# Linear attention with a decaying state, then top-128 expert routing: chunks of 64 tokens and 64x64x64 products instead of chunks of 128

## The chip, the core and the metric

The program runs on one core of a Trainium2 chip. The metric is the device time of one launch in microseconds. TensorE (PE) multiplies into PSUM, VectorE (DVE) and ScalarE (ACT) read PSUM, GpSimd (POOL) works on SBUF alone, and SyncE's queue (SP) issues nearly all transfers.

## What is computed

```python
B, H, S, D = 4, 8, 768, 64          # q, k, v; block = 64
for b in range(nb):
    intra = einsum('bhic,bhjc->bhij', qb, kb) * Dmask
    intra = einsum('bhij,bhjd->bhid', intra, vb)
    inter = einsum('bhid,bhde->bhie', qb * lam_pow, kv_state)
    out[:, :, sl] = intra + inter
    kv_state = lam_block * kv_state + einsum('bhsd,bhse->bhde', kb * rev_pow, vb)
x = out.transpose(0, 2, 1, 3).reshape(B, S, 512)
scores = einsum('bsd,d->bs', x, w_gate)
for b in range(B):                   # the 128 tokens with the highest score of each batch
    xe = x[b, top_idx]
    ye = maximum(xe @ w1, 0) @ w2    # 512 -> 1024 -> 512
    out[b, top_idx] = x[b, top_idx] + sigmoid(scores[b, top_idx])[:, None] * ye
```

All is float32. The chunk length is free, since the recurrence gives the same sums for any.

## The kernel before, in words

Tokens are worked in 24 tiles of 128 tokens (4 batches of 6), all 8 heads of a tile together. The order of every engine is the order in which the code is written (`manual_schedule`), and each engine takes its instructions strictly in that order. The loop over `g` at the end of the function is the pipeline. Step `g` issues the loads of tile `g+4` (three transfers of 256 KB, and in steps 0 to 3 two 512 KB pieces of the expert's weights as well), turns q and k of tile `g+2` round (`transposes`), takes the scores and the next state of tile `g+1` (`scores`, `next_state`), and the outputs of tile `g` (`outputs`). SP's queue holds the loads and the store of each tile in the same order.

Per tile, two heads make a pair `hp`. `scores` multiplies one head at a time: 64 rows of the array hold a head's keys, 128 columns its 128 tokens, and the two heads of a pair use the upper and the lower half of the array's rows. `mask` holds the powers of the decay for a 128x128 block. `next_state` multiplies keys by values for two heads at once and keeps the two useful 64x64 blocks of each 128x128 result; POOL decays the whole 128x512 state, zeros included, and DVE adds the blocks. `outputs` adds, per pair, one product with the state and two with the scores, in one PSUM bank `po`; ACT copies it to `x_b`, SP stores it, and DVE takes the gate's score (`xg`, `sc`).

`routing` ranks a batch's 768 scores once its last tile is done. PE spreads the scores over all partitions (`pb`), ACT copies them (`sc_row`), and DVE counts for every token how many come before it: two counting compares and a tie break for each of the 6 tiles (`count`, lines L265, L269, L273), three tiles in one step. `expert` then makes a 0/1 matrix out of the ranks (`pick`), PE turns it into row numbers (`pe`), POOL gathers the 128 rows (`xs`), and PE, ACT and DVE run the two layers (`gate` with `pt`, `hidden` with `ph`, `back` with `py` and `y`) before POOL scatters the rows back. `plan` spreads these pieces over the steps after the batch: counts at steps 6(b+1) and the next, `where` (pick and pe) 3 steps after 6(b+1), the gather one later, then `gate`, two `hidden`, two `back`, one a step. What is planned behind step 23 runs after the loop, with nothing beside it.

Of the kernel before, what the change touches and what calls it, by code (L numbers as in the profile page):

```python
# [17 lines left out]
def kernel(  # L18
# [18 lines left out]
    L = 128  # L37
    NT = S // L
# [5 lines left out]
    AHEAD = 4  # L44
# [4 lines left out]
    ld = ctx.enter_context(tc.tile_pool(name="ld", bufs=AHEAD + 3))  # L49
# [3 lines left out]
    ps_t = ctx.enter_context(tc.tile_pool(name="ps_t", bufs=1, space=PSUM))  # L53
    ps_s = ctx.enter_context(tc.tile_pool(name="ps_s", bufs=1, space=PSUM))
    ps_u = ctx.enter_context(tc.tile_pool(name="ps_u", bufs=1, space=PSUM))
    ps_o = ctx.enter_context(tc.tile_pool(name="ps_o", bufs=1, space=PSUM))
# [41 lines left out]
    mask = const.tile([128, H, L], FP32, name="mask")
    for h in range(H):
        nc.vector.tensor_tensor_scan(  # L100
            out=mask[:, h, :], data0=lam_b[:, h : h + 1].broadcast_to([128, L]),
            data1=ident[:], initial=0.0, op0=ALU.mult, op1=ALU.add,
        )

    kpow = const.tile([128, H], FP32, name="kpow")
    nc.vector.tensor_copy(kpow[:], mask[:, :, L - 1])  # L106
# [4 lines left out]
    for hh in range(2):  # L111
        r = slice(hh * 64, (hh + 1) * 64)
        nc.vector.tensor_copy(lam_p[r, :], lam_b[r, hh::2])
    qpow = const.tile([128, NHP, L], FP32, name="qpow")
    for hp in range(NHP):
        nc.vector.tensor_tensor_scan(
            out=qpow[:, hp, :], data0=lam_p[:, hp : hp + 1].broadcast_to([128, L]),
            data1=zero[:], initial=1.0, op0=ALU.mult, op1=ALU.add,
        )
    decay = const.tile([128, NHP, 128], FP32, name="decay")  # L120
    nc.vector.tensor_copy(decay[:], qpow[:, :, L - 1 : L].broadcast_to([128, NHP, 128]))

# [389 lines left out]
```

## Time and profile before

| | us |
|---|---|
| median of 3 runs | 250.05 (247.73 to 252.8) |
| the profiled execution | 248.36 |
| its span, first to last instruction | 246.7 |
| PE busy in it | 213.3 |
| DVE busy | 130.2 |
| POOL busy | 79.4 |
| ACT busy | 51.3 |
| mean granted TensorE clock | 0.939 of 2.4 GHz |

The profiled execution is one launch under the hardware profiler. Its time is 1.66 us longer than its span. Busy matmul time counts each pass until its result is out, and passes overlap, so PE's share says that it is seldom empty and not how fast it goes; the spacing of the passes tells that. A float32 matmul stands in the trace as two passes, each with its own weight load, so 16 passes are 8 matmuls.

### The profile page before, as it was taken

What the parts mean: (1) busy time and instruction counts of PE and PEld (TensorE: products, weight loads), DVE (VectorE), ACT (ScalarE), POOL (GpSimd) and SP (SyncE); (2) the same over time, 40 slices, a digit from 0 to 9 for tenths busy, and PEclk for the clock granted to TensorE, in tenths of its full rate; (3) what the DMA queues carried; (4) which work ended last, traced back from release to release, by engine and by line L of the source; (5) the groups of instructions that cost most, each with busy time, mean ns of one, the idle gap of its engine ahead of it and who ended that gap; (6) DMA issues with size and microseconds to landing.
All of it is one profiled execution on the core that took longest, in us unless ns stands there. A gap on an engine that the chain in (4) does not pass through costs nothing.

```text
span 246.7 us, 4281 instructions
## 1 busy us (share of the span) xinstructions
PE 213.3 (86%) x1664; PEld 182.8 (74%) x1664; DVE 130.2 (53%) x371; ACT 51.3 (21%) x97; POOL 79.4 (32%) x77
## 2 busy tenths in 40 slices
PE   1798998799877899999995999999997889817991
PEld 1598997589767799899682999899674877306940
DVE  4556453247999535299746244399644227821001
ACT  2312222223220123322120123412210022001000
POOL 1459641426644143254143144155131100030001
PEclk9999999799999799999998599999998899985897
DMA  6999999999955948917439159800101210020001
GB/s 130 218 228 250 224 299 279 284 257 249 239 134 115 214 115 179 203 24 170 113 59 213 43 127 201 188 27 18 44 30 55 88 43 0 0 79 9 0 0 43
DMA packets 80947, 31.99 MB, mean 130 GB/s; under 512 B 75680, under 2 KB 75680, under 8 KB 80928
## 3 DMA queue, kind: packets, MB, share of 16 engines
q1 hardware_dynamic: 80144, 29.63, 53.1%
q0 software_dynamic: 640, 2.10, 2.7%
q8 instruction: 13, 0.21, 0.4%
q14 instruction: 6, 0.05, 0.1%
q10 hardware_dynamic: 144, 0.00, 0.0%
HBM read 24.38 MB, written 7.34 MB: 129 GB/s over the span
## 4 chain that ended last, share of the span: by engine, by line
PE 53%; SPq 13%; DVE 11%; issue 10%; DMA 8%; ACT 2%; POOLq 1%
PE po L217 10%; SPq L68 10%; PE ph L360 9%; PE py L373 8%; PE ss L158 8%; DMA kn<-in_k_dram 7%; PE po L211 6%; PE pu L177 5%; PE tp_kT L133 3%; PE tp_qT L133 2%; DVE pick L299 2%; DVE p L164 2%; DVE cmp L269 2%; SPq L84 1%; DMA xs<-out_dram,tok 1%
## 5 line engine op out<-in xcount | busy, mean ns | idle before, releaser
L217 PE MATMUL po<-vn,p 128*128 128x64 f32 x384 | 53.5, 268 | 0.0
L141 POOL TENSOR_TENSOR qs<-qT,qpow 128x512 f32<-128x512 f32 x20 | 26.2, 1309 | 80.0 <-ACT qT L137 80.0
L217 PEld LDWEIGHTS po<-vn,p 128*128 128x128 f32 x384 | 51.4, 198 | 0.0
L164 DVE TENSOR_TENSOR p<-ss,mask 128x512 f32<-128x512 f32 x48 | 30.9, 685 | 25.2 <-PE ss L158 24.9
L211 PE MATMUL po<-state,qs 128*128 128x128 f32 x160 | 36.3, 310 | 0.8 <-ACT x_b L221 0.8
L221 ACT COPY x_b<-po 128x512 f32<-128x512 f32 x24 | 14.1, 587 | 104.7 <-PE po L217 104.7
L158 PE MATMUL ss<-qT,kT 64*128 64x128 f32 x384 | 32.9, 314 | 2.4 <-DVE p L164 2.2
L360 PE MATMUL ph<-xsT,w_sb 128*128 128x128 f32 x256 | 32.8, 291 | 1.4 <-ACT xsT L335 1.4
L360 PEld LDWEIGHTS ph<-xsT,w_sb 128*128 128x128 f32 x256 | 31.7, 206 | 2.1 <-ACT xsT L335 2.0
L158 PEld LDWEIGHTS ss<-qT,kT 64*128 64x128 f32 x384 | 27.4, 212 | 7.3 <-issue 3.8
L224 DVE CUSTOM_DVE_ANT_0 xg<-x_b,wg_b 128x512 f32<-128x512 f32 x24 | 17.1, 711 | 26.9 <-ACT x_b L221 26.6
L373 PE MATMUL py<-w_sb,hs 128*128 128x512 f32 x64 | 28.7, 596 | 0.0
L211 PEld LDWEIGHTS po<-state,qs 128*128 128x128 f32 x160 | 25.6, 202 | 1.7 <-issue 1.5
L177 PE MATMUL pu<-vn,kd 128*128 128x128 f32 x160 | 24.3, 297 | 0.6 <-DVE state L193 0.6
L145 POOL TENSOR_TENSOR kd<-kn,kpow 128x512 f32<-128x512 f32 x20 | 21.4, 1071 | 8.6 <-DVE kpow L106 5.4
L384 POOL DMA_INDIRECT out_dram<-y,tok x4 | 4.1, 1014 | 59.0 <-DVE pick L299 36.8
L177 PEld LDWEIGHTS pu<-vn,kd 128*128 128x128 f32 x160 | 20.4, 200 | 3.3 <-issue 0.8
L133 PE MATMUL tp_qT<-ident,qn 128*128 128x128 f32 x96 | 16.1, 294 | 7.7 <-DMA qn<-in_q_dram 7.7
L187 POOL TENSOR_TENSOR state<-state,decay 128x512 f32<-128x512 f32 x16 | 21.3, 1330 | 1.1 <-DVE state L193 1.1
L269 DVE TENSOR_SCALAR_CACHE_REDUCE cmp<-sc_row,sc 128x768 f32<-128x768 f32 (+5 forms) x24 | 16.2, 675 | 9.7 <-ACT sc_row L250 9.7
L373 PEld LDWEIGHTS py<-w_sb,hs 128*128 128x128 f32 x64 | 11.7, 190 | 12.4 <-issue 12.4
L137 ACT COPY qT<-tp_qT 128x512 f32<-128x512 f32 x24 | 14.1, 586 | 28.4 <-PE tp_qT L133 28.3
(56 smaller groups left out, 171.6 us busy)
## 6 DMA issues: line engine op xcount, KB each, us to landing
qn<-in_q_dram SPq DMA_DIRECT2D x24, 256.0 KB, 4.5
kn<-in_k_dram SPq DMA_DIRECT2D x24, 256.0 KB, 5.1
vn<-in_v_dram SPq DMA_DIRECT2D x24, 256.0 KB, 5.0
out_dram<-x_b SPq DMA_DIRECT2D x24, 256.0 KB, 2.2
w_sb<-in_moe_w_dram SPq DMA_DIRECT2D x8, 512.0 KB, 5.9
wg_b<-in_moe_w_gate_dram SPq DMA_DIRECT2D x1, 256.0 KB, 5.3
xs<-out_dram,tok POOLq DMA_INDIRECT x4, 3.4
out_dram<-y,tok POOLq DMA_INDIRECT x4, 2.8
```

Of the source, the lines that this page charges most:

```text
L68: nc.sync.dma_start(out=t[:], in_=src[b, :, rows, :].rearrange("h p d -> p h d"))
L133: nc.tensor.transpose(tp[:, hp, :], in_=t[:, 2 * hp : 2 * hp + 2, :], identity=ident[:])
L141: nc.gpsimd.tensor_tensor(out=qs[:], in0=qTs[g][:], in1=qpow[:], op=ALU.mult)
L145: nc.gpsimd.tensor_tensor(out=kd[:], in0=kn[:], in1=kpow[:].unsqueeze(2).broadcast_to([128, H, D]), op=ALU.mult,)
L158: nc.tensor.matmul(ss[hh][:, hp, :], lhsT=kT[r, hp, :], rhs=qT[r, hp, :], start=True, stop=True,)
L164: nc.vector.tensor_tensor(out=p[:, hh::2, :], in0=ss[hh][:], in1=mask[:, hh::2, :], op=ALU.mult)
L177: nc.tensor.matmul(pu[:, hp, :], lhsT=kd[:, 2 * hp : 2 * hp + 2, :], rhs=vn[:, 2 * hp : 2 * hp + 2, :].rearrange("p h e -> p (h e)"), star ...
L187: nc.gpsimd.tensor_tensor(out=new[:], in0=states[g][:], in1=decay[:], op=ALU.mult)
L211: nc.tensor.matmul(po[:, 2 * hp : 2 * hp + 2, :].rearrange("p h e -> p (h e)"), lhsT=qs[:, hp, :], rhs=state[:, hp, :], start=True, stop=F ...
L217: nc.tensor.matmul(po[:, h, :], lhsT=p[:, h, :], rhs=vn[:, h, :], start=(c == 0), stop=True, skip_group_check=True,)
L360: nc.tensor.matmul(ph[:, i, :], lhsT=w1_sb[:, dc, fs], rhs=xsT[:, dc, :], start=(dc == 0), stop=(dc == NDC - 1),)
L373: nc.tensor.matmul(py[:], lhsT=hs[:, fc, :], rhs=w2_sb[:, fc, :], start=(fc == 0), stop=(fc == NFC - 1),)
```

## The change

Three things change. First, the recurrence runs over chunks of 64 tokens, two to a tile. Every attention product becomes 64x64x64, one for each head and chunk, on one quarter of the array: a half of the rows (`hh` or the chunk) and a half of the columns. The four quarters of a pair are written one behind the other. There are now 16 matmuls of that shape for each of scores, state, state times queries and scores times values. Second, a state is stored as 128x256 without the zero blocks, and a tile has two state updates. Scores and state products of a step share one PSUM tile `su` of two banks with one buffer; `po` has two banks, the odd heads of the two chunks crossed over, so that ACT needs three copies for it. The transposes share the two buffers `pm` with the expert's tiles. Third, one compare a tile counts the rank, after all scores of a batch were rounded to a coarser grid by adding and taking off a constant (`steps`), and one instruction makes `pick`. The pieces are planned anew: the routing of batches 0 to 2 begins a step later, two counts a step, `back` in one piece, and an expert's pieces begin after those of the one before.

```diff
-    AHEAD = 4
+    AHEAD = 6
...
+    def quarters():
+        for hp in range(NHP):
+            for hh, c in ((0, 0), (1, 1), (1, 0), (0, 1)):
+                yield hp, hh, c
...
+    def scores(g, su):
...
+        for hp, hh, c in quarters():
+            nc.tensor.matmul(
+                su[half[c], hh, 0, hp, :], lhsT=kT[half[hh], hp, half[c]],
+                rhs=qT[half[hh], hp, half[c]], start=True, stop=True, skip_group_check=True,
+            )
...
+    def masked(g, su):
+        p = att.tile([128, 2, NHP, C], FP32, name="p")
+        nc.vector.tensor_tensor(
+            out=p[:].rearrange("p a b i -> p a (b i)"),
+            in0=su[:, :, 0].rearrange("p a b i -> p a (b i)"),
+            in1=mask[:].rearrange("p a b i -> p a (b i)"), op=ALU.mult,
+        )
...
+    def state_products(g, su):
+        vn, kd = loaded[g][2], kds.pop(g)
+        for hp, hh, c in quarters():
+            if c == 1 and g % NT == NT - 1:
+                continue
+            h = 2 * hp + hh
+            nc.tensor.matmul(
+                su[half[hh], c, 1, hp, :], lhsT=kd[half[c], h, :], rhs=vn[half[c], h, :],
+                start=True, stop=True, skip_group_check=True,
+            )
+
+    def decay_state(n):
...
+        t = att.tile([128, NHP, D], FP32, name="decayed", bufs=2)
+        nc.gpsimd.tensor_tensor(out=t[:], in0=states[n][:], in1=decay[:], op=ALU.mult)
...
+    def next_state(n, su):
...
+            nc.vector.tensor_tensor(out=new[:], in0=u, in1=decayed.pop(n)[:], op=ALU.add)
...
+    def from_states(g):
...
+                po[half[hh ^ c], hh, hp * D : (hp + 1) * D],
+                lhsT=qs[half[hh], hp, half[c]], rhs=states[n][half[hh], hp, :],
+                start=(hp == 0), stop=False, skip_group_check=True,
+            )
...
+    def from_scores(g):
...
+                po[half[hh ^ c], hh, hp * D : (hp + 1) * D],
+                lhsT=p[half[c], hh, hp, :], rhs=vn[half[c], 2 * hp + hh, :],
...
+        nc.scalar.copy(out=x_b[:, t, :, 0, :], in_=po[:, 0])
+        for c in range(2):
+            nc.scalar.copy(out=x_b[half[c], t, :, 1, :], in_=po[half[1 - c], 1])
...
                 nc.vector.scalar_tensor_tensor(
...
+                    out=cmp[:], in0=keep["sc_row"][:], scalar=scs[b][:, t : t + 1],
+                    in1=earlier[:, (NT - 1 - t) * L : (NT - 1 - t) * L + S],
+                    op0=ALU.subtract, op1=ALU.is_gt, accum_out=keep["rank"][:, t : t + 1],
                 )
...
+            nc.vector.tensor_tensor(
+                out=pick[:],
+                in0=slots[:, r0 : r0 + 128].unsqueeze(1).broadcast_to([128, NT, 128]),
+                in1=rank[:].unsqueeze(2).broadcast_to([128, NT, 128]), op=ALU.is_equal,
+            )
...
-        s = (b + 1) * NT
+        s = (b + 1) * NT + (b < B - 1)
...
-            put(s + i // 3, piece)
+            put(s + i // 2, piece)
...
+        start_su(g)
+        su = sus.pop(g)
         if g + 2 < NG:
-            transposes(g + 2)
+            decay_state(2 * g + 4)
+        if g + 3 < NG:
+            keys_decayed(g + 3)
+        from_scores(g)
+        outputs(g)
         if g + 1 < NG:
-            scores(g + 1)
-            next_state(g + 1)
-        outputs(g)
+            from_states(g + 1)
+            scores(g + 1, su)
+        if g + 2 < NG:
+            state_products(g + 2, su)
+        if g + 1 < NG:
+            masked(g + 1, su)
+        if g + 2 < NG:
+            next_state(2 * g + 4, su)
+            decay_state(2 * g + 5)
+        gate_scores(g)
+        if g + 2 < NG:
+            next_state(2 * g + 5, su)
+        if g + 3 < NG:
+            transposes(g + 3, "qT", qTs)
+            queries_decayed(g + 3)
         if g % NT == NT - 1:
             plan(g // NT)
         for piece in later.pop(g, []):
             piece()
+        if g + 3 < NG:
+            transposes(g + 3, "kT", kTs)
```

In this code `half[i]` is partitions or tokens 64i to 64i+63, a chunk `n` is half a tile, and the work between two chunks is a chain: state products on PE, the add on DVE, the decay on POOL, the next add.

A step on PE, before (tp are the transposes, ss the scores, pu the state products, po the outputs; the four rows of the ss pair and of po that repeat are left out):

```order
L133 MATMUL tp_qT<-ident,qn 128x128 x4
L133 MATMUL tp_kT<-ident,kn 128x128 x4
L158 MATMUL ss_1717<-qT,kT 128x128
L158 MATMUL ss_1718<-qT,kT 128x128
...
L177 MATMUL pu<-vn,kd 128x128 x4
L211 MATMUL po<-state,qs 128x128
L217 MATMUL po<-vn,p 128x64 x2
```

And now, with the numbers-to-rows step of batch 1 in it (step 16; su holds scores and state products, pick and pe turn the ranks into row numbers):

```order
L243 MATMUL po<-vn,p 64x64 x16
L230 MATMUL po<-state,qs 64x64 x16
L176 MATMUL su<-qT,kT 64x64 x16
L196 MATMUL su<-vn,kd 64x64 x16
L154 MATMUL tp_qT<-ident,qn 128x128 x4
L337 LDWEIGHTS pick
L337 MATMUL pe<-place,pick 128x2
...
L154 MATMUL tp_kT<-ident,kn 128x128 x4
```

A step's 56 passes become 136. The transposes of tile g+3 end the step instead of beginning it, and pe stands between its two halves, where before it stood ahead of both.

DVE at the routing of a batch (batch 2), before (p is the masked scores, xg the gate's score):

```order
L260 MEMSET parts 128x1
L269 TENSOR_SCALAR cmp,parts<-sc_row,sc 128x768
L273 SCALAR_TENSOR_TENSOR cmp,parts<-sc_row,sc,below 128x128
L265 TENSOR_SCALAR cmp,parts<-sc_row,sc 128x128
L269 TENSOR_SCALAR cmp,parts<-sc_row,sc 128x640
L273 SCALAR_TENSOR_TENSOR cmp,parts<-sc_row,sc,below 128x128
L265 TENSOR_SCALAR cmp,parts<-sc_row,sc 128x256
L269 TENSOR_SCALAR cmp,parts<-sc_row,sc 128x512
L273 SCALAR_TENSOR_TENSOR cmp,parts<-sc_row,sc,below 128x128
L164 TENSOR_TENSOR p<-ss_1633,mask 128x4x128
L164 TENSOR_TENSOR p<-ss_1634,mask 128x4x128
```

And now (batch 0):

```order
L217 TENSOR_TENSOR state<-su,decayed 128x256
L315 TENSOR_SCALAR sc<-sc 128x6
L305 SCALAR_TENSOR_TENSOR cmp,rank_1154<-sc_row,sc,earlier 128x768 x2
L183 TENSOR_TENSOR p<-su,mask 128x512
L217 TENSOR_TENSOR state<-su,decayed 128x256
L267 ISA xg,sc<-x_b,wg_b 128x512
L267 ISA sc 128x1
L217 TENSOR_TENSOR state<-su,decayed 128x256
L305 SCALAR_TENSOR_TENSOR cmp,rank_1154<-sc_row,sc,earlier 128x768 x2
```

Between the masked scores of two steps stood eight counting instructions, and now stand two.

PE where the loop ends, before (the last rows of the attention, then the expert of batch 2):

```order
L211 MATMUL po<-state,qs 128x128
L217 MATMUL po<-vn,p 128x64 x2
L331 MATMUL pt<-ident,xs 128x128 x4
L360 MATMUL ph<-xsT,w_sb 128x128 x16
L245 MATMUL pb<-ident,sc 128x128 x6
L360 MATMUL ph<-xsT,w_sb 128x128 x16
L373 MATMUL py<-w_sb,hs 128x512 x8
```

And now:

```order
L176 MATMUL su<-qT,kT 64x64 x16
L337 LDWEIGHTS pick
L337 MATMUL pe<-place,pick 128x2
...
L243 MATMUL po<-vn,p 64x64 x16
L363 MATMUL pt<-ident,xs 128x128 x4
L288 MATMUL pb<-ident,sc 128x128 x6
L392 MATMUL ph<-xsT,w_sb 128x128 x32
L403 MATMUL py<-w_sb,hs 128x512 x8
```

Batch 2's pe stood two tiles ahead of the last outputs, before the scores of tile 23 (not shown). Now 16 matmuls, the outputs of tile 23, stand between it and pt, which needs the gathered rows.

## Rows read from the trace of the kernel before

**Rows 1.** Stretches: length; busy PE, PEld, DVE, ACT, POOL; clock; DMA share; GB/s.

```profile
0.00:63.90 63.90, 54.28 (x471) 49.15 (x472) 32.81 (x89) 16.94 (x30) 30.20 (x34) 0.97 1.08 243
63.90:81.80 17.90, 13.60 (x121) 11.95 (x119) 17.26 (x48) 3.73 (x7) 8.07 (x6) 1.00 0.69 154
81.80:131.80 50.00, 49.62 (x411) 43.32 (x410) 28.52 (x78) 12.39 (x24) 17.10 (x15) 0.97 0.62 136
131.80:143.00 11.20, 8.57 (x55) 7.61 (x56) 5.21 (x12) 1.17 (x2) 3.10 (x3) 0.70 0.41 95
198.10:246.70 48.60, 34.60 (x180) 24.81 (x178) 15.11 (x58) 5.15 (x11) 2.95 (x3) 0.86 0.06 22
```

**Rows 2.** Timeline of PE, one step (18) with nothing else: start, us, line.

```profile
168.01 0.60 PE L133 MATMUL tp_qT<-ident,qn 128*128 128x128 f32 x4
168.98 1.16 PE L158 MATMUL ss<-qT,kT 64*128 64x128 f32 x16
170.07 1.16 PE L177 MATMUL pu<-vn,kd 128*128 128x128 f32 x8
171.07 0.39 PE L211 MATMUL po<-state,qs 128*128 128x128 f32 x2
...
173.69 0.65 PE L373 MATMUL py<-w_sb,hs 128*128 128x512 f32 x1
```

**Rows 3.** The same timeline, asked up to 169.6 and to 170.6 us.

```profile
168.98 0.83 PE L158 MATMUL ss<-qT,kT 64*128 64x128 f32 x10
170.07 0.71 PE L177 MATMUL pu<-vn,kd 128*128 128x128 f32 x4
```

**Rows 4.** Groups by line and shape: busy us, mean ns; then idle before.

```profile
L164 DVE TENSOR_TENSOR p<-ss,mask 128x512 f32<-128x512 f32 x48 | 30.9, 685 | 25.2 <-PE ss L158 24.9
L224 DVE CUSTOM_DVE_ANT_0 xg<-x_b,wg_b 128x512 f32<-128x512 f32 x24 | 17.1, 711 | 26.9 <-ACT x_b L221 26.6
L193 DVE TENSOR_TENSOR state<-pu,state 64x256 f32<-64x256 f32 x32 | 13.4, 420 | 11.3 <-POOL state L187 11.1
L269 DVE TENSOR_SCALAR_CACHE_REDUCE cmp<-sc_row,sc 128x768 f32<-128x768 f32 x4 | 4.0, 1012 | 9.7 <-ACT sc_row L250 9.7
L145 POOL TENSOR_TENSOR kd<-kn,kpow 128x512 f32<-128x512 f32 x20 | 21.4, 1071 | 8.6 <-DVE kpow L106 5.4 <-DMA kn<-in_k_dram 3.2
L141 POOL TENSOR_TENSOR qs<-qT,qpow 128x512 f32<-128x512 f32 x20 | 26.2, 1309 | 80.0 <-ACT qT L137 80.0
L187 POOL TENSOR_TENSOR state<-state,decay 128x512 f32<-128x512 f32 x16 | 21.3, 1330 | 1.1 <-DVE state L193 1.1
```

**Rows 5.** Views of two tiles, cmp and pick: ns min/median/max.

```profile
L273 DVE SCALAR_TENSOR_TENSOR cmp<-sc_row,sc,below x24: 350/352/1046, 60.2 to 213.8; 128x128 f32<-128x128 f32 x24
L299 DVE TENSOR_SCALAR pick<-slots,rank x24: 274/278/1802, 80.4 to 216.5; 128x128 bf16<-128x128 f32 x24
```

**Rows 6.** Chain that ended last, 131 to 142 us: start, us, what.

```profile
132.57 2.51 DVE pick L299 x5
...
135.51 1.00 PE tp_qT L133 x4
...
137.36 2.01 PE ss L158 x16
```

**Rows 7.** Timeline, end of the loop and the last batch's gather and expert.

```profile
197.85 0.61 PE L331 MATMUL pt<-ident,xs 128*128 128x128 f32 x4
199.18 3.84 PE L360 MATMUL ph<-xsT,w_sb 128*128 128x128 f32 x32 [0.72 <-ACT xsT L335]
207.74 7.03 PE L373 MATMUL py<-w_sb,hs 128*128 128x512 f32 x16
217.52 0.15 DVE L317 CAST tok<-tok_f 128x1 int32<-128x1 f32 x1
222.81 1.12 PE L331 MATMUL pt<-ident,xs 128*128 128x128 f32 x4 [5.72 <-DMA xs<-out_dram,tok]
224.60 9.96 PE L360 MATMUL ph<-xsT,w_sb 128*128 128x128 f32 x64 [0.67 <-ACT xsT L335]
```

More of the change, by code (lines that the diff above doesn't have):

```diff
@@ L93 @@
     make_identity(nc, ident)
-    zero = const.tile([128, L], FP32, name="zero")
+    ident2 = const.tile([128, C], FP32, name="ident2")
+    nc.vector.tensor_tensor(out=ident2[:], in0=ident[:, :C], in1=ident[:, C:], op=ALU.add)
+    zero = const.tile([128, C], FP32, name="zero")
     nc.vector.memset(zero[:], 0.0)
[L98 to L103, printed above, removed]
@@ L105 @@
-    kpow = const.tile([128, H], FP32, name="kpow")
-    nc.vector.tensor_copy(kpow[:], mask[:, :, L - 1])
+    half = [slice(0, C), slice(C, 2 * C)]
+    mask = const.tile([128, 2, NHP, C], FP32, name="mask")
+    for hh in range(2):
+        for hp in range(NHP):
+            h = 2 * hp + hh
+            nc.vector.tensor_tensor_scan(
+                out=mask[:, hh, hp, :], data0=lam_b[:, h : h + 1].broadcast_to([128, C]),
+                data1=ident2[:], initial=0.0, op0=ALU.mult, op1=ALU.add,
+            )
@@ new lines, in transposes, with queries_decayed @@
+    def transposes(g, name, keep):
+        t = loaded[g][0 if name == "qT" else 1]
+        tp = ps_m.tile([128, NHP, L], FP32, name="tp_" + name, tag="pm")
+        for hp in range(NHP):
+            nc.tensor.transpose(
+                tp[:, hp, :], in_=t[:, 2 * hp : 2 * hp + 2, :], identity=ident[:]
+            )
+        dst = att.tile([128, NHP, L], FP32, name=name)
+        nc.scalar.copy(out=dst[:], in_=tp[:])
+        keep[g] = dst
+    def queries_decayed(g):
+        qs = att.tile([128, NHP, L], FP32, name="qs")
+        nc.gpsimd.tensor_tensor(
+            out=qs[:], in0=qTs[g][:], in1=qpow[:].rearrange("p a c i -> p a (c i)"), op=ALU.mult
+        )
+        qss[g] = qs
@@ L198, in outputs @@
     def outputs(g):
[L199 to L202 removed]
+        b, t = divmod(g, NT)
+        if t == 0:
+            x_bs[b] = xpool.tile([128, NT, NHP, 2, D], FP32, name="x_b")
             scs[b] = xpool.tile([128, NT], FP32, name="sc")
[L204 to L207 removed]
@@ new lines, in do, with steps @@
+                    in1=earlier[:, (NT - 1 - t) * L : (NT - 1 - t) * L + S],
+                    op0=ALU.subtract, op1=ALU.is_gt, accum_out=keep["rank"][:, t : t + 1],
+                )
+            return do
+        n = (NT + 1) // 2
+        def steps():
+            nc.vector.tensor_scalar(
+                out=scs[b][:], in0=scs[b][:], scalar1=2.0 ** -100, scalar2=2.0 ** -100,
+                op0=ALU.add, op1=ALU.subtract,
+            )
+        first = [steps] + [rows(t0, min(n, NT - t0)) for t0 in range(0, NT, n)]
@@ L291, in expert @@
+        return keep, first, [count(t) for t in range(NT)]
     def expert(b, r0, keep):
```

282 lines of the change are left out of this document (121 added, 161 removed).

## The prediction

> **What bounds the kernel now.** I read the table of stretches first [rows 1]. It shows four regimes. Up to 63.9 us (the first transpose of step 8) the loads are the limit with PE close behind: the DMA engines are busy all the time (share 1.08) at 243 GB/s, while PE is busy for 54.3 of 63.9 us. From 63.9 to 81.8 us DVE is the limit (17.3 of 17.9 us, PE 13.6): there the ranks of batch 0 are counted. From 81.8 us PE is the limit (49.6 of 50.0 us), but for the two places where PE stands idle until `pick` is made; one of them is in 131.8 to 143.0, with PE at 8.6 of 11.2 us and a mean clock of 0.70. Behind 198.1 us is the tail of 48.6 us: the expert of batch 2, then gather and expert of batch 3, one thing after the other.
>
> The timeline of one step on PE [rows 2] gives prices at the full clock. The reader should look at starts and not at busy times, since passes overlap. A step takes 173.69 - 168.01 = 5.68 us. How far apart passes stand shows where the same row is cut short [rows 3]: the scores' passes 11 to 16 add 1.16 - 0.83 = 0.33 us, 55 to 56 ns a pass, and the state products' passes 5 to 8 add 1.16 - 0.71 = 0.45 us, 112 ns a pass. Both have 128 columns each way. The scores' passes use half of the array's rows, two heads side by side, and that makes them twice as fast. 16 x 0.056 = 0.90 us and the next row begins 1.09 us after the scores' start; 8 x 0.112 = 0.90, and the outputs begin 1.00 us after the state products' start. So a change from one array shape to another costs 0.1 to 0.2 us. The 8 transposes take 168.98 - 168.01 = 0.97 us with such a change, 0.88 without.
>
> **PE's attention work.** The change takes away 48 passes a step and puts 128 in their place, in four groups of 32 (scores, state products, queries times states, scores times values), each pass with 64 weight columns and 64 moving columns on a quarter of the array. No row shows a quarter. The nearest row is the scores': two row halves side by side, 128 columns each way, 56 ns a pass. With half the columns and only the two row halves side by side a pass costs 28 ns; that is what I take. The lower end is 14 ns (the column halves side by side as well). The upper end is 56 ns: the spacing doesn't follow the columns at all. At 28 ns a group is 0.90 us, and a step 4 x 0.90 + 8 transposes (0.88) + two changes of shape at 0.1 = 4.7 us in place of 5.68.
>
> **The stretch to step 8.** Step 7 now ends with the k transposes of tile 10, which need 11 tiles of 0.786 MB, 4.2 MB of expert weights, 0.26 MB of gate weights and the 4 stores queued ahead of them: 14.1 MB, at 243 GB/s 58 us, and I take 60 for the landing. PE alone would need some 15 us for the first three tiles and 8 x 4.7, which is less. So 60 us where it was 63.9.
>
> **Steps 8 to 23.** They hold 57.5 groups (16 of scores times values, 14 of queries times states since the first chunk of a batch has none, 15 of scores, 12.5 of state products): 51.8 us. Transposes of 13 tiles and changes of shape: 11.4 + 2.6. The expert pieces of batches 0 and 1 stay: `ph` 4 x 3.65 [rows 7], `py` 2 x 7.0 [rows 7], some 4.2 for `pt`, `pb` and `pe`: 32.8 us. Sum 98.6 us. The same account of before is 114.4 us of the 134.2 between 63.9 and 198.1 us; the other 19.8 are waits and a low clock.
>
> What becomes of these waits? DVE's counting falls: in place of three instructions a tile (the 768-wide one 1.01 us [rows 4]) one of the form whose 128-wide case takes 0.35 [rows 5], so by 640 more elements at the rate of the 768-wide row about 1.05 to 1.1; two a step instead of six or more. A step then costs DVE one 0.69 (half the masking), two state adds of 0.42, 0.79 for `xg` and 2.3 for counts [rows 4]: 4.6 us, just inside PE's 4.7. That ends the DVE-bound stretch. But `pick` stays in PE's way, and more than before. `pe` now stands between the two transposes of a step, and `pick` waits on DVE behind masking, first add, `xg` and second add. The masking now waits for the state products as well (in the order it alone waits for PE, the adds only for POOL). From the end of the state products that is 0.3 + 0.69 + 0.42 + 0.77 + 0.42 + about 1.0 for `pick`, less 0.54 of q transposes: 3.1 us of idle PE in steps 10 and 16, 2.9 in step 22, and 1.0 together for the share of DVE's instructions that are stretched while POOL works (0.35 became up to 1.05, 0.28 up to 1.8 [rows 5]). Queued behind `pe` are the k transposes and the whole next step. After such a wait the clock drops: at 135.51 four transposes took 1.00 us for 0.44 and the scores 2.01 for 0.9 [rows 6], 2 to 2.7 us lost each time: 6.6 for three. `pt` waits about 1 us each for the gathers of batches 0 and 1, which are queued on POOL behind kd and qs, and `pb` in step 7 waits 2.2 us for the last `xg` and `steps`. Together 98.6 + 10.1 + 6.6 + 2 + 2.2 = 119.5 us, for 134.2.
>
> **The tail.** Before, batch 2's rows were there when the last outputs ended, and `pt` followed at 197.85 without a wait [rows 7]. Now its `pick` comes in step 22 and only the last 0.9 us of PE work stand between `pe` and `pt`. From the end of `tok` to `pt` the last batch took 222.81 - 217.67 = 5.1 us [rows 7], and `tok` itself is ready about when these 0.9 us end. So 5.1 us of idle PE that weren't there, and the clock falls: `pt` 1.12 for 0.61, and 64 passes of `ph` took 9.96 us after the same wait, where 32 took 3.84 [rows 7], so 3 us more. One `pick` of 1.0 for six saves 0.4. Tail 48.6 + 8.1 - 0.4 = 56.3 us.
>
> **Edits that I cost at nothing.** POOL gets a second, half as wide decay (about 0.66, from 1.33), and kd and qs for all 24 tiles: 1.07 + 1.31 + 2 x 0.66 = 3.7 us a step [rows 4], under PE's 4.7; were a step shorter than that, POOL would be late next. ACT's three copies for one are under 1.2 us, ACT being idle for most of a step; SP's stores and the loads behind them wait for that, but the loads run six tiles ahead. The rounding (0.15 us), the new tables and the scans lie in stretches where loads are the limit. The transposes in the shared `pm` buffers wait for one ACT copy, made while other passes run.
>
> **The sum.** 60 + 119.5 + 56.3 = 235.8 us of span, 237.5 with the 1.66 around it, against 248.36. The median of the runs shown is 250.05, 0.7% over the profiled execution, so the forecast is 239 us, 4.4% less. A measurement of this kernel can tell about 2%.
>
> **Rivals.** First, the column halves overlap too, 14 ns a pass. The 57.5 groups lose 0.45 each: 26 us. But then PE reaches its waits sooner: from the end of the state products to the next scores stand masking, an add, a decay or `xg`, and the second add, 2.8 us, and PE has only 2.1 us of other work; and the waits at `pick` grow by the time that PE comes earlier. About 10 to 11 us go there: 224 us. For it speaks that two row halves do run side by side; against it that no row shows column halves. The Trainium skill, TensorEngine Tiling (Array Packing), Key Properties, says that tiles run loads and matmuls independently and in parallel, which would be this rival; its Gotcha 1 says that different row tiles can't use one PSUM bank at once, which neighbours in `from_scores` do. The trace has no quarter to agree or disagree. The Trainium skill, TensorE: Matmul & The Clock Gate (Wait — 56ns, not 53.3ns?), says that starts never come closer than about 25 ns; an estimate by it is 0.8 us a group and 235 us, and no row here shows passes closer on average than 56.
>
> Second, slower: a pass with its weight load can't follow the last one in less than the 56 ns of the scores, whatever its columns, because the number of passes and not their width sets the pace. A group is 1.79 us, a step 8.2. Steps 8 to 23 grow by 57.5 x 0.89 = 51 us, the first eight steps become PE's (15 + 8 x 8.2 = 81 for 60), and some 4 us of waits are covered: 307 us. It decides from about 34 ns a pass, where 57.5 x 0.19 = 11 us eat the gain. For it: PE's passes go from 56 to 136 a step, and the trace has none that are narrow both ways. Against it: passes of 128 columns run at 112 ns on all rows and at 56 on halves [rows 3], so their number alone doesn't set the pace.
>
> Third, no change: PE is as forecast and DVE is not. With POOL busy for 3.7 us of each 4.7, the counts and picks of batches 0 to 2, which read two SBUF operands, mostly take the long form: 18 counts by 0.7 [rows 5], of which half shows in PE's waits, and 0.5 more at each `pick`: 8 us, 247.
>
> **How the numbers follow.** Forecast 0.40, column halves 0.26, no change 0.12, slower 0.22. The range leaves out most of the slower case and little of the fast one: 222 to 262, the top being 37 ns a pass. The forecast's own range is 232 to 245. Faster by over 2% (under 245): the first rival and nearly all of the forecast, 0.64. Within 2%: 0.15. Slower: 0.21.
>
> **What would show it.** In the profile after, the spacing of the 64x64 passes decides: 32 passes in 0.45, 0.9 or 1.8 us. DVE should have no stretch of its own behind 60 us. PE should stand idle for about 3 us before `pe` in steps 10, 16 and 22, and for about 5 before the first `pt` of the tail. The prediction fails if the passes go at another pace, or if a step is bound by the chain masking, add, decay, add.

## The result, and the profile after

The changed kernel takes 238.4 us (median of 4 runs, 237.9 to 238.7) where the kernel before took 249.8 beside it: 0.957 times, 95% interval 0.951 to 0.963. The forecast was 239, in the range 222 to 262. The number is right, and three of the steps that lead to it are not. The profiled execution took 238.65 us, with a span of 236.9. Some executions are a few per cent slower than others of the same kernel; the times here and below are medians of all, the ratios leave the slow ones out.

The table of stretches of the changed kernel answers to [rows 1] (length; busy PE, PEld, DVE, ACT, POOL; clock; DMA share; GB/s):

```profile
0.00:68.90 68.90, 42.99 (x1202) 36.36 (x1202) 26.74 (x83) 22.90 (x48) 42.87 (x50) 0.85 0.99 231
61.20:68.90 7.70, 3.56 (x18) 2.53 (x18) 1.67 (x3) 1.54 (x3) 4.67 (x5) 0.50 0.98 229
68.90:181.50 112.60, 89.32 (x2143) 74.74 (x2142) 65.56 (x130) 37.15 (x84) 59.96 (x51) 0.86 0.57 133
181.50:236.90 55.40, 35.56 (x184) 25.94 (x180) 11.37 (x30) 5.83 (x13) 4.39 (x4) 0.81 0.08 24
```

| Stretch | before | predicted | after |
|---|---|---|---|
| to step 8 | 63.9 | 60 | 68.9 |
| steps 8 to 23 | 134.2 | 119.5 | 112.6 |
| tail | 48.6 | 56.3 | 55.4 |
| span | 246.7 | 235.8 | 236.9 |

The first stretch is longer than before, and PE's mean clock is lower in all three (it was 0.97, 0.95 and 0.86 of full speed before); the second row is the first one's end. The timeline of PE shows why. It answers to [rows 2, 3] (start, us, line; in brackets the idle time before, and what ended it):

```profile
112.33 0.69 PE L243 MATMUL po<-vn,p 64*64 64x64 f32 x32
112.85 0.65 PE L230 MATMUL po<-state,qs 64*64 64x64 f32 x32
113.32 0.65 PE L176 MATMUL su<-qT,kT 64*64 64x64 f32 x32
113.78 0.65 PE L196 MATMUL su<-vn,kd 64*64 64x64 f32 x32
114.36 0.65 PE L154 MATMUL tp_qT<-ident,qn 128*128 128x128 f32 x4
```

The third and the fourth group begin 0.47 and 0.46 us after the one ahead of them, which is 14.5 ns a pass: all four quarters of the array work at once (e1_one below has the pace of one by itself, about 60 ns). That is the first rival's price, not the forecast's 0.90 us a group. A whole step's attention is 2.0 us. But PE now runs into waits, and this is the same view at other places (answers to [rows 6, 7]):

```profile
27.44 0.33 PE L230 MATMUL po<-state,qs 64*64 64x64 f32 x2 [1.37 <-issue]
38.33 0.33 PE L230 MATMUL po<-state,qs 64*64 64x64 f32 x4 [2.54 <-issue]
61.16 1.09 PE L154 MATMUL tp_qT<-ident,qn 128*128 128x128 f32 x4 [3.83 <-DMA qn<-in_q_dram]
66.38 1.51 PE L288 MATMUL pb<-ident,sc 128*128 128x128 f32 x6 [4.14 <-DVE sc L315]
68.87 1.14 PE L243 MATMUL po<-vn,p 64*64 64x64 f32 x32
69.78 1.08 PE L230 MATMUL po<-state,qs 64*64 64x64 f32 x32
87.72 0.32 PE L337 MATMUL pe<-place,pick 128*128 128x2 bf16 x6 [6.08 <-DVE pick L330]
100.67 1.09 PE L363 MATMUL pt<-ident,xs 128*128 128x128 f32 x4 [3.38 <-DMA xs<-out_dram,tok]
136.20 0.32 PE L337 MATMUL pe<-place,pick 128*128 128x2 bf16 x6 [3.75 <-DVE pick L330]
180.62 0.30 PE L337 MATMUL pe<-place,pick 128*128 128x2 bf16 x6 [2.90 <-DVE pick L330]
185.72 1.12 PE L363 MATMUL pt<-ident,xs 128*128 128x128 f32 x4 [4.17 <-DMA xs<-out_dram,tok]
213.46 1.11 PE L363 MATMUL pt<-ident,xs 128*128 128x128 f32 x4 [6.45 <-DMA xs<-out_dram,tok]
```

The waits stand where the prediction put them: before `pe` in steps 10, 16 and 22, and before `pt`. In steps 10 and 16 they are longer, 6.1 and 3.75 us for some 3.1. Behind a wait a group takes 0.85 to 0.91 us in place of 0.47 (68.87 to 69.78): PE's clock has gone from 2.4 GHz to 1.2 (0.50 of full speed in the row of 61.2 to 68.9 us, where PE worked 3.6 of 7.7 us).

The groups answer to [rows 4] (busy us, mean ns; then the idle time before them):

```profile
L206 POOL TENSOR_TENSOR decayed<-state,decay 128x256 f32<-128x256 f32 x40 | 39.6, 989 | 38.5 <-DVE state L217 32.5 <-DVE state L215 6.0
L217 DVE TENSOR_TENSOR state<-su,decayed 128x256 f32<-128x256 f32 x40 | 16.8, 419 | 21.2 <-POOL decayed L206 21.2
L230 PE MATMUL po<-state,qs 64*64 64x64 f32 x704 | 19.6, 237 | 7.9 <-issue 7.8
```

The half-wide decay takes 0.99 us in the mean where 0.66 was estimated, and DVE waited 21 us for it. `cmp` and `pick`, which answer to [rows 5], depend on what POOL does (views of the two tiles, ns min/median/max):

```profile
L305 DVE SCALAR_TENSOR_TENSOR cmp<-sc_row,sc,earlier x24: 1008/1018/2028, 68.4 to 194.9; 128x768 f32<-128x768 f32 x24
L330 DVE TENSOR_TENSOR pick<-slots,rank x4: 949/1308/1661, 86.0 to 205.7; 128x768 bf16<-128x768 f32 x4
```

The timelines of DVE and POOL where batch 0 is counted show how a `cmp` of 1.0 us becomes one of 2.0:

```profile
79.76 2.03 DVE L305 SCALAR_TENSOR_TENSOR cmp<-sc_row,sc,earlier 128x768 f32<-128x768 f32 x1
81.72 1.78 DVE L305 SCALAR_TENSOR_TENSOR cmp<-sc_row,sc,earlier 128x768 f32<-128x768 f32 x1
```

```profile
79.16 1.82 POOL L163 TENSOR_TENSOR qs<-qT,qpow 128x512 f32<-128x512 f32 x1
80.93 1.76 POOL L143 TENSOR_TENSOR kd<-kn,kpow 128x512 f32<-128x512 f32 x1
```

The two engines take turns. `cmp` of 79.76 seems to get on when `qs` ends (80.98): it ends 0.8 us after that, and takes 1.0 in all where it meets nothing. `kd`, there from 80.93, ends 1.0 us (its time by itself) after that `cmp` (82.69 for 81.7); the next `cmp` ends 0.8 us after `kd`. State adds and masking, which read PSUM, keep their 0.42 and 0.69 us there. The Trainium skill, SBUF — State Buffer (Who interferes with whom), says that a DVE instruction with two SBUF inputs contends with a POOL instruction that reads SBUF, and that the port pair they share is an exclusive lock. The rows agree: 1.0 us becomes 2.0.

### The profile page after: what moved, and what is told of

It reads as the page before. It is cut to its first block, busy times and chain, and to the rows that moved or that the text cites. A ratio compares the mean times of both kernels' runs of the same rounds, so it can differ in the third digit from the quotient of the medians.

```text
span 236.9 us, 7953 instructions
## 1 busy us (share of the span) xinstructions
PE 167.9 (71%) x3520; PEld 137.0 (58%) x3520; DVE 103.7 (44%) x241; ACT 65.9 (28%) x145; POOL 107.2 (45%) x105
## 4 chain that ended last, share of the span: by engine, by line
PE 43%; DMA 21%; issue 13%; DVE 12%; POOL 6%; SPq 2%; ACT 1%; POOLq 1%
DMA kn<-in_k_dram 15%; PE ph L392 10%; PE py L403 9%; DMA xs<-out_dram,tok 6%; PE po L243 4%; PE su L196 4%; PE su L176 4%; DVE cmp L305 4%; PE tp_kT L154 3%; PE po L230 3%; POOL decayed L206 3%; PE tp_qT L154 2%; POOL kd L143 2%; DVE pick L330 2%; DVE p L183 2%
## 5 line engine op out<-in xcount | busy, mean ns | idle before, releaser
L206 POOL TENSOR_TENSOR decayed<-state,decay 128x256 f32<-128x256 f32 x40 | 39.6, 989 | 38.5 <-DVE state L217 32.5
L183 DVE TENSOR_TENSOR p<-su,mask 128x512 f32<-128x512 f32 x24 | 16.6, 691 | 42.0 <-PE su L196 37.0
L305 DVE SCALAR_TENSOR_TENSOR cmp<-sc_row,sc,earlier 128x768 f32<-128x768 f32 x24 | 28.5, 1229 | 9.7 <-ACT sc_row L293 9.7
L154 PE MATMUL tp_qT<-ident,qn 128*128 128x128 f32 x96 | 19.2, 332 | 10.1 <-DMA qn<-in_q_dram 10.0
L217 DVE TENSOR_TENSOR state<-su,decayed 128x256 f32<-128x256 f32 x40 | 16.8, 419 | 21.2 <-POOL decayed L206 21.2
L230 PE MATMUL po<-state,qs 64*64 64x64 f32 x704 | 19.6, 237 | 7.9 <-issue 7.8
L176 PE MATMUL su<-qT,kT 64*64 64x64 f32 x768 | 21.1, 249 | 5.4 <-DVE state L217 4.0
L176 PEld LDWEIGHTS su<-qT,kT 64*64 64x64 f32 x768 | 18.1, 159 | 6.8 <-issue 6.6
L230 PEld LDWEIGHTS po<-state,qs 64*64 64x64 f32 x704 | 16.6, 152 | 8.8 <-issue 8.5
L196 PE MATMUL su<-vn,kd 64*64 64x64 f32 x704 | 21.0, 257 | 0.4 <-issue 0.3
L243 PE MATMUL po<-vn,p 64*64 64x64 f32 x768 | 18.9, 244 | 1.3 <-DVE p L183 1.3
L154 PEld LDWEIGHTS tp_qT<-ident,qn 128*128 128x128 f32 x96 | 12.5, 168 | 12.2 <-issue 10.4
```

The source lines that it names most:

```text
L154: nc.tensor.transpose(tp[:, hp, :], in_=t[:, 2 * hp : 2 * hp + 2, :], identity=ident[:])
L176: nc.tensor.matmul(su[half[c], hh, 0, hp, :], lhsT=kT[half[hh], hp, half[c]], rhs=qT[half[hh], hp, half[c]], start=True, stop=True, skip_g ...
L196: nc.tensor.matmul(su[half[hh], c, 1, hp, :], lhsT=kd[half[c], h, :], rhs=vn[half[c], h, :], start=True, stop=True, skip_group_check=True,)
L206: nc.gpsimd.tensor_tensor(out=t[:], in0=states[n][:], in1=decay[:], op=ALU.mult)
L230: nc.tensor.matmul(po[half[hh ^ c], hh, hp * D : (hp + 1) * D], lhsT=qs[half[hh], hp, half[c]], rhs=states[n][half[hh], hp, :], start=(hp ...
L243: nc.tensor.matmul(po[half[hh ^ c], hh, hp * D : (hp + 1) * D], lhsT=p[half[c], hh, hp, :], rhs=vn[half[c], 2 * hp + hh, :], start=(hp == ...
```

## Experiments

Each kernel ran beside the kernel before, whose median was 249.8 to 253.3 us on the chips used; the ratio is to the kernel before on the same chip.

| Kernel | us | ratio (95%) |
|---|---|---|
| changed | 238.4 | 0.957 (0.951 to 0.963) |
| e1_rows | 241.8 | 0.965 (0.953 to 0.978) |
| e1_one | 265.3 | 1.063 (1.051 to 1.076) |
| e2_after_oldcounts | 239.6 | 0.961 (0.947 to 0.976) |
| e2_before_newcounts | 251.4 | beside 252.2 |
| e3_pe | 237.3 | 0.946 (0.938 to 0.954) |
| e4_tail | 228.0 | 0.913 (0.902 to 0.924) |
| e5_order | 236.8 | 0.948 (0.937 to 0.959) |
| e6_all | 222.6 | 0.890 (0.879 to 0.901) |
| e7_fix | 215.7 | 0.867 (0.850 to 0.884) |
| e8_few_loads | 223.6 | 0.896 (0.883 to 0.910) |
| e9_act | 231.5 | 0.923 (0.899 to 0.947) |
| e10_dve_states | 213.1 | 0.847 (0.834 to 0.861) |

For e2_before_newcounts there is no ratio: its runs (244 to 256) and those of before beside it (248 to 262) scatter too much.

**What a pass costs.** The order of the 32 passes is changed, and each of the four groups maps array row half r and column half k to its own hh and c.

```diff
-            for hh, c in ((0, 0), (1, 1), (1, 0), (0, 1)):
-                yield hp, hh, c
+        for k in range(2):
+            for hp in range(NHP):
+                for r in range(2):
+                    yield hp, r, k
```

> The changed kernel with its 32 passes of a group in another order: neighbours differ in the array's row half and stay in one column half for 16 passes; nothing else differs. Theory A (row halves and column halves each double the pace, and what PE gained is partly given back in waits): a pass goes from 14.5 to about 28 ns, a group from 0.47 to 0.9 us; the 57.5 groups of steps 8 to 23 grow by 25 us, of which the waits of these steps take up 8 to 13, so 250 to 256 us. Rival (another engine or the loads set the pace of the steps): the groups grow alike, and the time stays under 244. If the group stays at 0.47 us, the column halves do not matter and the time is 238.

In the second kernel the loops stand as k, r, hp:

> The changed kernel with the passes of a group ordered quarter by quarter: eight passes on one quarter, then eight on the next. Theory A: nothing runs side by side, a pass is half of the 112 ns of 128 columns, 56 ns, a group 1.8 us, a step without expert pieces 8.2 us; steps 8 to 23 grow by 57.5 x 1.33 = 76 us less some 20 of waits that are covered, the first eight steps become PE's (+12): 295 to 310 us, where the prediction put its second rival (307). Rival (a pass of 64 columns is cheap by itself, and the halves do not matter): a group stays near 0.5 us and the time near 238.

Measured: 241.8 and 265.3 us. PE's timeline of e1_rows, where each group shows its first row only, and then of e1_one, asked up to 102.12, up to 102.17 and up to 107 us:

```profile
96.22 0.80 PE L248 MATMUL po<-vn,p 64*64 64x64 f32 x26
...
96.81 0.27 PE L234 MATMUL po<-state,qs 64*64 64x64 f32 x2
```

```profile
101.94 0.38 PE L248 MATMUL po<-vn,p 64*64 64x64 f32 x3
...
101.94 0.44 PE L248 MATMUL po<-vn,p 64*64 64x64 f32 x4
...
103.09 0.27 PE L234 MATMUL po<-state,qs 64*64 64x64 f32 x1
...
104.24 0.27 PE L178 MATMUL su<-qT,kT 64*64 64x64 f32 x1
```

One quarter by itself takes a pass every 0.06 us (0.44 - 0.38); eight of them are about the 0.47 us in which the changed kernel does all four quarters. So four quarters go at four times the pace of one. Row halves double it ([rows 3]), and so the column halves must double it as well, as theory A has it. My group times were wrong for both (0.9 and 1.8 expected, 0.59 and 1.15 measured), because the passes of the next half or quarter start while the last ones of this one still wait, as the rows of two groups lying in one another show. The times follow: a group that is 0.12 us longer costs 3.4 us in all (within the scatter of the two kernels), one that is 0.68 longer costs 27. In steps 8 to 23 these are 7 and 39 us of PE work, so the waits take up about half of the first and a third of the second. e1_rows alone lies where the rival put it, under 244; that something else sets the pace of every step falls with the 27 us of e1_one. Near 14.5 ns much of PE's pace is covered.

**Quarters or counts.** The old counting (three instructions a tile, six for `pick`) in the changed kernel, and the new one in the kernel before:

```diff
+                nc.vector.tensor_scalar(
+                    out=cmp[:, t * L :], in0=sc_row[:, t * L :], scalar1=s, scalar2=None,
+                    op0=ALU.is_gt, op1=ALU.add, accum_out=parts[:, 1, t : t + 1],
+                )
                 nc.vector.scalar_tensor_tensor(
-                    out=cmp[:], in0=keep["sc_row"][:], scalar=scs[b][:, t : t + 1],
...
+                    out=cmp[:, t * L : (t + 1) * L], in0=sc_row[:, t * L : (t + 1) * L],
...
```

> The changed kernel with the routing of the kernel before: three counting instructions a tile and six for pick; attention in quarters. Theory A: DVE is later by 0.7 to 1 us a tile where batch 0 is counted and by about 1 at each pick: 242 to 247 us. Rival D (the counts bring the gain, the quarters nothing): about 250.

> The kernel before with nothing of the change but the routing: one rank compare per 128 tokens, the rounding of the scores and one instruction for pick; attention as before in passes of 128 columns. Theory A (quarters bring most of the gain): the DVE-bound stretch of batch 0 shrinks by up to 4 us and each wait for pick by about 1: 242 to 247 us. Rival D (the counts bring the gain): 238 to 240.

Measured: 1.2 us more with the old counting, and 0.8 less than before with the new one, neither beyond what these runs can tell. So the gain comes from the rest of the change, and e1_one shows that there is none without the quarters side by side. What the deeper prefetch (`AHEAD`), the narrower state and the new order of a step bring or cost by themselves, no run shows. The counts were expected to bring 3 us or more either way and did not. A part of the reason stands in the traces: the old wide compares have one SBUF input and keep their time beside POOL (0.34 to 1.01 us, as before), while a new one that meets POOL takes up to 2.0; DVE counted batch 0 from 65.5 to 78.6 us with the old ones and from 68.4 to 83.5 with the new.

**The waits.** Three reorderings, one by one and then together. First `pe` one step behind `pick`:

```diff
             put(s + 1, with_rank if i else where)
+            d = 1 if b < B - 2 else 0
+            put(s + 1 + d, on_pe)
             put(s + 2, fetch)
             for j, piece in enumerate(pieces):
-                put(s + 3 + j, piece)
+                put(s + 3 + d + j, piece)
```

> The changed kernel with pe of batches 0 and 1 one step behind its pick (steps 11 and 17), the gather issued in that same step and everything behind it one step later. Theory A (what the quarters freed is given back where PE runs into a wait of the routing): the waits of 6.1 and 3.75 us before pe and of 3.4 and 2.6 us before pt go, and some 4 us of low clock behind them; a part comes back as waits for the masking, since DVE is busy without a gap while batch 0 is counted: 8 to 14 us less than the changed kernel, 225 to 230 us. Rival C (POOL and the chain of states set the pace of a step, PE only waits somewhere else): 235 to 239.

Measured: 237.3 us, 1.1 less, which is within the scatter and where rival C put it. Theory A falls for these waits. PE's timeline of e3_pe shows what came in their place (`pe` itself had no wait at 89.00 us):

```profile
84.11 0.69 PE L243 MATMUL po<-vn,p 64*64 64x64 f32 x32 [2.09 <-DVE p L183]
86.17 1.13 PE L176 MATMUL su<-qT,kT 64*64 64x64 f32 x32 [0.91 <-DVE state L217]
98.02 0.69 PE L176 MATMUL su<-qT,kT 64*64 64x64 f32 x32 [2.36 <-DVE state L217]
104.34 1.51 PE L288 MATMUL pb<-ident,sc 128*128 128x128 f32 x6 [2.96 <-DVE sc L315]
```

DVE has work almost without a gap from 74.9 to 87.7 us (12.2 of 12.8 in the changed kernel), so PE waits for the masking instead; `pb` of batch 1 now meets the gate of batch 0.

In the tail, batch 2's routing goes a step earlier, and batch 3's counts, `pick`, `pe` and gather go ahead of batch 2's last product:

```diff
+        if b == B - 1:
+            later[NG][:0] = first + counts + [where]
+            put(NG + 1, on_pe)
+            put(NG + 1, fetch)
+            t = [NG + 3 + j for j in range(len(pieces))]
+        elif b == B - 2:
+            for i, piece in enumerate(first + counts):
+                put(NG - NT + max(0, i - len(first)) // 2, piece)
+            put(NG - 4, where)
+            put(NG - 3, on_pe)
+            put(NG - 2, fetch)
+            t = [NG - 1 + j for j in range(len(pieces))]
...
```

> The changed kernel with batch 2's routing one step earlier (its rows are gathered while step 22 and 23 run) and batch 3's counts, pick, pe and gather ahead of batch 2's last product; batches 0 and 1 as they are. Theory A: of the tail's waits (2.9 before pe in step 22, 4.2 before pt, 1.2 before pb, 1.7 before pe, 6.45 before pt) 12 to 15 us go, and 1 to 3 us of low clock: 221 to 227 us. Rival (the tail is bound by one chain of counts, gather and expert whatever the order): 233 to 239.

Measured: 228.0 us, 10.4 less. PE's timeline of e4_tail has the last batch without its two waits:

```profile
183.70 1.11 PE L367 MATMUL pt<-ident,xs 128*128 128x128 f32 x4 [4.69 <-DMA xs<-out_dram,tok]
196.07 0.29 PE L341 MATMUL pe<-place,pick 128*128 128x2 bf16 x6
203.59 0.60 PE L367 MATMUL pt<-ident,xs 128*128 128x128 f32 x4
```

Batch 2's `pt` still waits 4.7 us: its gather stands on POOL behind batch 1's scatter, which waits for `py`. That is why it missed the 12 to 15 us.

Third, the order inside a step (first state add ahead of the masking, `xg` last; `kd` behind both decays):

```diff
-        if g + 3 < NG:
-            keys_decayed(g + 3)
         from_scores(g)
...
-        if g + 1 < NG:
-            masked(g + 1, su)
         if g + 2 < NG:
             next_state(2 * g + 4, su)
             decay_state(2 * g + 5)
-        gate_scores(g)
+        if g + 3 < NG:
+            keys_decayed(g + 3)
+        if g + 1 < NG:
+            masked(g + 1, su)
         if g + 2 < NG:
             next_state(2 * g + 5, su)
+        gate_scores(g)
```

> The changed kernel with another order on DVE and POOL inside a step: first state add, then the masking, second add, xg; and on POOL both decays before kd. Theory: in step 7 the second decay no longer queues behind kd, which waits for the load of tile 10 until 63.1 us, so step 8 starts 2 to 3.5 us earlier; and where scores wait for the second state add (0.5 to 0.9 us in some six steps) the wait shrinks by 0.4: 232 to 236 us. Rival (kd, now later on POOL, holds up the state products): 238 to 242.

Measured: 236.8 us, 1.6 less, within the scatter (3.3 less in the profiled execution). `pb` of step 7 does come at 61.9 us where it came at 66.4, and `pe` of step 10 at 83.1 for 87.7, behind a wait of 5.5 us. The forecast of this run was a little low; the trace shows its mechanism.

> The last three together (pe and gather of batches 0 and 1 a step later, the tail's order, the order inside a step). Theory A: the gains add up but for what the steps' own chain (state add, decay, state add, and POOL's 4.4 us a step) takes back: 203 to 215 us. Rival C (POOL and the chain of states set the pace): only the tail's gain is left, 222 to 228.

Measured: 222.6 us, 15.8 less. The number lies in rival C's range, but not for its reason, that only the tail's gain is left (10.4): the three gains alone add up to 13.1, and together they bring no less. Theory A's range came from gains that were each put too high, e3_pe's above all. Two more moves on POOL's and PE's queues (`put(NG - 3, fetch)` for batch 2, and the score rows ahead of the gate):

> The version with the three reorderings together, and two more: batch 2's gather stands ahead of batch 1's scatter on POOL (there it waited for py, so pt stood idle for 7.4 us), and batch 1's score rows stand ahead of batch 0's gate (pb waited 3.0 us behind it on DVE). Theory (the wait at pt is the order on POOL's queue): 7 us and 2 of low clock go in the tail and 1 to 3 in step 13: 209 to 215 us. Rival (PE only waits somewhere else, POOL and the chain of states set the pace): 219 to 222.

Measured: 215.7 us, 7.0 less. The order on POOL's queue was the cause of batch 2's wait at `pt`, which was 7.4 us in e6_all and is gone; the wait at batch 1's `pb` stayed (3.4 us), and so did one of 5.8 at batch 2's.

**Loads and POOL.**

```diff
+        if g > AHEAD:
+            loaded[g] = first_tiles[g % (AHEAD + 1)]
+            return
```

> The changed kernel with loads for its first seven tiles only; tiles 7 to 23 are computed from these seven again (this leaves out 13.4 MB of loads). Theory B (up to step 8 the loads set the end, whatever PE does): the first transpose of step 8's tile comes 12 to 20 us earlier, at PE's and POOL's pace of 3.5 to 4.5 us a step, and the time is 218 to 226 us; the gaps of 1.4 to 2.5 us in the middle of a group of passes between 25 and 50 us, which stand where a block of instructions is fetched while the DMA engines are full, go too. Rival C (POOL and the chain of states set the pace there as well): step 8 starts no more than 5 us earlier, 233 to 237 us.

Measured: 223.6 us, 14.8 less than the changed kernel. Tile 10 is transposed at 55.6 us, where it was 61.2, and `pb` comes at 59.3 where it was 66.4. So loads do set the end of that stretch, but with 5.6 to 7.1 us and not 12 to 20, because POOL is next. Its timeline in e8_few_loads has no gap for two steps once the loads are in:

```profile
48.10 1.11 POOL L209 TENSOR_TENSOR decayed<-state,decay 128x256 f32<-128x256 f32 x1 [2.76 <-DVE state L220]
49.16 1.27 POOL L166 TENSOR_TENSOR qs<-qT,qpow 128x512 f32<-128x512 f32 x1
50.39 0.73 POOL L209 TENSOR_TENSOR decayed<-state,decay 128x256 f32<-128x256 f32 x1
51.07 1.05 POOL L146 TENSOR_TENSOR kd<-kn,kpow 128x512 f32<-128x512 f32 x1
52.13 1.12 POOL L209 TENSOR_TENSOR decayed<-state,decay 128x256 f32<-128x256 f32 x1
```

A step is 4.03 us of POOL there (52.13 - 48.10). The other 8 us of the gain I did not take apart; the mean clock is 0.91 for 0.85, and 4.1 of them lie between `pt` and the first `ph` of batches 0 and 1 (5.0 and 3.5 us, where it was 6.3 twice).

```diff
-        nc.gpsimd.tensor_tensor(out=t[:], in0=states[n][:], in1=decay[:], op=ALU.mult)
+        for hp in range(NHP):
+            nc.scalar.activation(
+                t[:, hp, :], states[n][:, hp, :], AF.Copy, scale=decay[:, hp, 0:1]
+            )
```

> The changed kernel with the decay of the states on ACT (four instructions of 64 columns, scaled by a value per partition) instead of POOL; nothing else differs. Theory C (POOL's 4.4 us a step, and DVE instructions with two SBUF inputs that are stretched while POOL runs, set the pace of steps 8 to 17): POOL loses 40 us, cmp goes from 1.23 to about 1.1 us, the waits of scores for the state add shrink: 228 to 234 us. Theory A (the places of the routing's waits and the loads do): 236 to 240. Rival (four instructions of about 0.25 us in ACT's queue lengthen the chain add, decay, add): 240 to 246.

Measured: 231.5 us, 6.9 less, in theory C's range, although an instruction on ACT took 0.34 us. `cmp` stayed at 1.25 us, so fewer collisions with `cmp` are not the gain. PE's timeline of e9_act shows where it lies:

```profile
62.72 1.33 PE L291 MATMUL pb<-ident,sc 128*128 128x128 f32 x6 [0.38 <-DVE sc L318]
81.92 0.32 PE L340 MATMUL pe<-place,pick 128*128 128x2 bf16 x6 [5.35 <-DVE pick L333]
```

In the changed kernel these stand at 66.38 and 87.72. So of the 6.5 us between the profiled executions 3.7 were won by step 7, where the decay no longer queues behind `kd` (the chain that e5_order moves as well), 2.1 more while batch 0 was counted (0.7 of them in `pick`, which took 0.95 us for 1.66), and only 0.7 behind that. That POOL sets the pace of all steps up to 17, as theory C has it, is not shown.

```diff
-            nc.vector.tensor_tensor(out=new[:], in0=u, in1=decayed.pop(n)[:], op=ALU.add)
+            for hp in range(NHP):
+                nc.vector.scalar_tensor_tensor(
+                    out=new[:, hp, :], in0=old[:, hp, :], scalar=decay[:, hp, 0:1],
+                    in1=u[:, hp, :], op0=ALU.mult, op1=ALU.add,
+                )
```

> The version with the five reorderings, and decay and add of a state in one step on DVE: four instructions of 64 columns (old state by a value per partition, plus the product from PSUM) in place of a decay on POOL and an add on DVE; masking first again. Theory C (POOL in the chain of the states costs what remains): POOL loses 33 us, the hop from DVE to POOL and back goes, and fewer DVE instructions meet POOL: 203 to 209 us against 215.7. Rival (eight instructions of some 0.25 us are 1.2 us more of DVE in each step, and DVE takes POOL's place): 214 to 218.

Measured: 213.1 us, between the two ranges, 2.6 less than e7_fix and within their intervals. Eight instructions take 1.6 us on DVE, so DVE seems to take over most of POOL's place; this reading is argued and not tested. This is the fastest kernel, 0.85 of before.

## Why the prediction was right, and where it was wrong

**The pass price** is the step that failed: "with half the columns and only the two row halves side by side a pass costs 28 ns; that is what I take". It is 14.5, since the column halves overlap as well. [Rows 3] showed row halves, the prediction had no row of column halves and took the nearer row over the rival. In steps 8 to 23 this is 57.5 x (0.90 - 0.47) = 25 us too much PE work. The Trainium skill, TensorEngine Tiling (Array Packing), Key Properties, by which tiles work independently and in parallel, was right here. Its Gotcha 1 would have slowed `from_scores`, whose neighbours write one PSUM bank from different row halves; that group takes 0.52 us, the others 0.46 to 0.58. The Trainium skill, TensorE: Matmul & The Clock Gate (Wait — 56ns, not 53.3ns?), has starts no closer than about 25 ns. Between quarters that does not hold: they are 14.5 ns apart on average.

**The waits and what surrounds them** were under-priced by nearly as much. All that is not groups of passes in steps 8 to 23 was put at 119.5 - 51.8 = 67.7 us and took 112.6 - 26.8 = 85.8, or 18 more (20 without the 2.2 us for `pb` in step 7, which lie in the table's first stretch and were 4.1 there). The rows give 12.7 for `pe` (10.1 said, with the stretching) and 6.0 for `pt` (2 said). Five times the four groups behind a wait run at the low clock and take 3.6 us for 2.0, some 8 us together without the transposes beside them (6.6 said for all, at three places); waits for masking and state adds are 3.4 us. The rest is not taken apart. The first rival saw this: "the waits at `pick` grow by the time that PE comes earlier", but put it at 10 to 11 us.

So the number came out by luck: 25 us too much for the groups, against 18 too little for what surrounds them and 9 too little for the first stretch. At the forecast's own price the kernel would not have taken 239 us: between e1_rows (0.59 us a group, 18.4 ns a pass, 241.8 us) and e1_one (1.15 us, 36 ns, 265.3 us) the straight line gives an estimate of 255 at 28 ns, no gain at all. (The price of a nanosecond seems to grow, from 0.9 us below e1_rows to 1.3 above; by the flatter one it is 250 at 28 ns, still none.) The break-even of 34 ns was too high as well; by these estimates 250 is reached at 25 to 28.

**The stretch to step 8** came to 68.9 us for 60. The loads landed 1 to 3 us later than worked out (`qn` of tile 10 let PE go on at 61.2 us, `kn` let POOL go on at 63.3), and behind them stood a chain that I did not see. The timelines of POOL and DVE have it:

```profile
63.26 1.04 POOL L143 TENSOR_TENSOR kd<-kn,kpow 128x512 f32<-128x512 f32 x1 [5.79 <-DMA kn<-in_k_dram]
64.26 0.72 POOL L206 TENSOR_TENSOR decayed<-state,decay 128x256 f32<-128x256 f32 x1
65.02 0.42 DVE L217 TENSOR_TENSOR state<-su,decayed 128x256 f32<-128x256 f32 x1 [6.01 <-POOL decayed L206]
65.36 0.87 DVE L315 TENSOR_SCALAR sc<-sc 128x6 f32<-128x6 f32 x1
```

`kd` waits for `kn` on POOL, ahead of the second decay of step 7, on which the state add, the rounding `steps` and `pb` (66.38) wait. In e5_order, where `kd` stands behind that decay, `pb` comes 4.5 us earlier.

**Edits costed at nothing.** POOL was: "were a step shorter than that, POOL would be late next". It was, and it was (e8_few_loads; in e9_act it shows in step 7 above all). The half-wide decay was under-priced by a half (0.99 for 0.66); the shortest in e8_few_loads' rows take 0.73, so most of the excess probably comes where DVE and POOL meet. "DVE should have no stretch of its own behind 60 us" is wrong: 74.9 to 87.7 us is one. The third rival's mechanism, DVE contended with POOL, is real and was part of the forecast's error; the gain of the counts went at least in part into it.

**The tail** was right in size (56.3, measured 55.4) and in cause: `pt` waited 4.2 us (5.1 said) for the gather that the delayed routing of batch 2 laid open; POOL issued it at 181.8 us, when `tok` had just come. With the routing a step earlier the gather met the scatter on POOL and the wait stayed (4.7 us in e4_tail, whose gain is mostly the last batch's); with both moved it was gone (e7_fix).

## What to carry to other kernels

When one engine gets several times faster at its main work, price the next chain (here load, POOL, DVE and back) before the gain, since PE's waits grow by the time that it comes earlier. A wait that is moved to another step is worth only what the engine it waits for has idle: the moves that clearly paid were those in the tail, where DVE and POOL had nothing else to do. Where a range rests on whether two things run side by side, ask what each order of the passes would do; the order alone was worth 27 us here.

## What the runs showed that I had not expected

Although PE is given its instructions strictly in the order of the code, passes of different quarters overtake one another in the trace, so that even the order quarter by quarter runs at 36 ns a pass and not at the 60 or so of one quarter.

PE stands idle in the middle of a group, where nothing waits for data (1.37 and 2.54 us [<-issue] above; 7.8 us in five places). The gaps stand in the same places in nearly all kernels with this program, some 125 passes apart, which with their weight loads are 250 instructions. The page of the changed kernel has this row for the fetch of instructions, where before it was 13 packets and 0.21 MB:

```profile
q8 instruction: 28, 0.46, 0.8%
```

The Trainium skill, Runtime: NRT & Kernel Launch (Instruction fetch mechanics), says that blocks of 256 instructions are fetched while the last ones run, and that this is mostly hidden. Here it seems not to be, where 125 passes take under 3 us: in the trace one packet of that queue stands 2.3 to 3.2 us ahead of PE's next pass in each of the five places. In e8_few_loads the gaps were not gone: one of 3.4 us ended at 45.7, while the loads were still coming in, and one of 1.3 at 54.2, behind all loads. So the fetch probably sets a pace of its own. That is argued from the places of the gaps and not shown, and how much of the first stretch it costs stays open; no kernel here had the same work in fewer instructions.

A DVE instruction can be passed over more than once: one `xg` (two SBUF inputs, 0.68 us alone) took 2.90 us at 98.75 in the changed kernel, while three POOL instructions ran behind one another to 101.1.
